# Four 16-bit score buffers instead of two for VectorE's exponentials, longer GpSimd products in the plan, and a new order

## The chip, the cores and the metric

The kernel runs on one core of a Trainium2 chip. A core has five engines that run side by side, each with its own instruction stream executed in order: TensorE (PE, matrix multiply), VectorE (DVE), ScalarE (ACT, activation functions), GpSimd (POOL) and SyncE (SP, here only a queue that starts DMA transfers). Engines wait for each other through semaphores. Matmul results land in PSUM, eight banks of 2 KB per partition; everything else lives in SBUF. The metric is the device time of one execution in microseconds (us), the median of several runs. A profile records every instruction of one execution.

## The reference

Two layers, each an attention block and an MLP block, on one sequence of 2048 rows of 448 values, 16 heads of 28:

```python
def _A_ref(x, wqkv, wo):            # attention
    q, k, v = split(x @ wqkv)       # 16 heads of 28
    scores = einsum("bhqd,bhkd->bhqk", q, k) * (28 ** -0.5)
    p = softmax(scores, axis=-1)
    return merge(einsum("bhqk,bhkd->bhqd", p, v)) @ wo

def _B_ref(x, w1, w2, w3, w4):      # shift mixer and MLP
    h = gelu(layernorm(x) @ w1)     # tanh form
    hs = shift_rows(h in four column groups, by -1, +1, -2, +2) @ w2
    x1 = x + hs
    return x1 + gelu(layernorm(x1) @ w3) @ w4

for _ in range(2):
    x = x + _A_ref(layernorm(x), wqkv, wo)
    x = x + _B_ref(layernorm(x), w1, w2, w3, w4)
```

In total 2 x 16 x 2048 x 2048 exponentials are needed, and they are the largest elementwise job of the program.

## The kernel before, in words

**Tiles.** The sequence is 16 row tiles of 128. Queries are cut into chunks of 4, 4, 4, 2 and 2 tiles (`CHUNKS`), heads into four groups `g` of four. A *segment* is one chunk, one head group and a range of key tiles; `ORDER` lists the ranges, for layer 0 `(0, 0, 4), (1, 0, 4), (0, 4, 8), (0, 8, 16), (1, 4, 16), (2, 0, 16), ...`, each for four head groups. There are 68 segments. A *block* is one 512-column score tile (128 keys by 512 query columns, of one head, or two key tiles by 256 columns in the short chunks); there are 2048 blocks.

**Exponentials on two engines.** `t_scores` groups blocks into units. TensorE writes the scores of a unit into banks 0 to 2 or 3 to 4 (5 at times), and one ScalarE instruction (line 1754, in `t_exp`) computes the exponential of two or three blocks at once into the ring `PT`. Some blocks go to VectorE instead. `ahead_of` chooses one from 5 to 9 steps further on, if the planner's rates (`R_RATE`, `D_RATE`, one entry for two segments) allow it and if a `y` buffer, a `pd` buffer and a bank are free at once (`"try"`). `d_first` (line 1584) reads the scores from PSUM into a 16-bit integer tile `y`; `d_chain` (lines 1611 to 1624) then computes the exponential from integer and bf16 operations, seven instructions on 512 columns, each dependent on one before it. Its scratch is an `f` buffer (2 KB, shared with other work: normalization and gelu) and, before the change, the second half of the 2 KB `y` buffer, which holds the tile `w`. While parts of the value store `vaug` are still unused, its slots serve as further buffers (`xtra`, `t_extra`).

**After the scores.** `t_pv` multiplies the exponentials with the values into one bank (line 831); at the end of each segment VectorE copies or adds the sum into `ub` (lines 1838 and 1840). `t_norm` brings the row sums by DMA to one tile, takes reciprocals, broadcasts them back by DMA into an `f` buffer (line 1861) and multiplies (`otn`, line 1865). `t_outproj`, `t_mixA`, `t_mixB` and `t_w4` do the output projection and the mixer and MLP of the finished rows beside the attention of the next chunks. What they still have to do for the last chunks runs after the last exponential; the second row group of the MLP there is tiles 11 and 12, the third 13 to 15.

**Products on GpSimd or VectorE.** `both(key, pool_dur, dve_dur, ...)` places a product of two SBUF tiles by `XPAR[key]`: 1 for VectorE, 0 for GpSimd, 2 for the one that would end it first by the plan. This holds for `otn` (key `eo`), the squares of queries and keys (`eq`, `ek`), the squares in gelu (`ez`, line 2034) and the addition `x_res + x1b` (`ex`, line 2120).

**The order.** No order is written by hand. Every piece of work is a Python generator, and `Sched.run` picks the next instruction of each engine at build time, with a planned duration for each, ranks (`RANK`, and `dp`, `rp` in `XPAR`), leads (`Q_LEAD`) and thresholds (`dt`, `wt`, `ft`). `after_lock` keeps a VectorE instruction marked `two` and a long GpSimd product from overlapping in the plan. Where the plan leaves TensorE a gap, `keep_pe_busy` puts in filler matmuls (line 2267) that no result depends on. `Plan.finalize` turns dependencies into semaphore waits. The engines then execute their lists in that order, whatever the real durations are.

## Time and profile before

| | before |
|---|---|
| median of 3 runs | 1025.69 us (1025.05 to 1025.9) |
| profiled execution | 1025.66 us |
| its span | 1023.9 us |
| instructions | 36349 |
| TensorE busy | 973.4 us, 95% |
| ScalarE busy | 973.6 us, 95% |
| VectorE busy | 843.5 us, 82% |
| GpSimd busy | 220.1 us, 21% |
| exponentials on ScalarE (line 1754) | 791 instructions, 877.8 us |
| score tiles read by VectorE (line 1584) | 94 into `yd`, 40 into `vaug` |
| filler matmuls | 2508 |

In a row of the groups stand: source line, engine, operation, what is written and read, count, then total busy time, mean duration of one in ns, and the idle time of the engine just before these instructions with what ended it. Durations of neighbours on one engine overlap a little, so a mean is longer than the step from one start to the next. In a row of the timeline stand start and length in us, and in brackets the idle time before it and its releaser. The granted TensorE clock is shown as a share of full speed.

### The profile page before, as it was taken

The numbers are of one execution on the slowest core, as the hardware profiler recorded it, in microseconds if no ns is written. First come the engines' busy times: TensorE is split into PE (matmuls) and PEld (weight loads), VectorE is DVE, ScalarE is ACT, GpSimd is POOL, SyncE is SP. The second block draws the span as 40 slices with busy tenths as digits, with TensorE's granted clock in tenths as the row PEclk, the third lists the DMA queues.
The fourth block names the chain that finished last, engine by engine and source line by source line (L and its number), as shares of the span: only waits on it lengthen the run. The fifth ranks groups of instructions, "written<-read, shape, count | busy, mean of one in ns | idle before, by whom it ended". The sixth has DMA issues, their size and how long they took to land.

```text
span 1023.9 us, 36349 instructions
## 1 busy us (share of the span) xinstructions
PE 973.4 (95%) x16102; PEld 404.7 (40%) x16102; DVE 843.5 (82%) x2134; ACT 973.6 (95%) x897; POOL 220.1 (21%) x350
## 2 busy tenths in 40 slices
PE   8999899999999999999999999999999999999998
PEld 4333344334343334344344333333333333444465
DVE  8879999988768778897788888997898888788752
ACT  6899999999999999999999999999999999999942
POOL 4003022143213013350212010112332200331220
PEclk9999999999999999999999999999999999999999
DMA  4534228121203113321133024324311110220000
GB/s 126 130 74 140 59 76 216 34 44 37 33 18 84 43 49 88 51 39 19 36 87 63 22 76 140 112 80 112 74 29 33 32 55 13 55 61 17 13 21 25
DMA packets 98829, 64.43 MB, mean 63 GB/s; under 512 B 70832, under 2 KB 87552, under 8 KB 98672
## 3 DMA queue, kind: packets, MB, share of 16 engines
q1 hardware_dynamic: 94176, 53.11, 21.1%
q0 software_dynamic: 3376, 8.09, 3.0%
q8 instruction: 126, 2.06, 0.9%
q10 hardware_dynamic: 1120, 0.92, 0.3%
q14 instruction: 31, 0.25, 0.1%
HBM read 28.16 MB, written 16.76 MB: 44 GB/s over the span
## 4 chain that ended last, share of the span: by engine, by line
ACT 62%; PE 23%; DVE 12%; DMA 1%; issue 1%; ACTq 0%; SPq 0%; DVEq 0%
ACT PT L1754 55%; PE ps L840 12%; PE ps L1487 5%; PE ps L831 4%; ACT h2T L2220 3%; PE ps L2267 1%; ACT fb L2036 1%; DVE yd L1584 1%; DMA xT<-xnd 1%; DVE fb L1619 1%; DVE fb L1615 1%; DVE PD L1624 1%; DVE ub L1840 1%; DVE vaug L1621 1%; ACT L1754 1%
## 5 line engine op out<-in xcount | busy, mean ns | idle before, releaser
L1754 ACT ACTIVATE PT<-ps 128x1024 bf16<-128x1024 f32 (+1 forms) x791 | 877.8, 1288 | 7.8 <-PE ps L1487 6.6
L1487 PE MATMUL ps<-qT,kT 32*128 32x512 bf16 (+1 forms) x2560 | 310.1, 340 | 23.5 <-ACT PT L1754 17.7
L831 PE MATMUL ps<-PT,vaug 128*32 128x512 bf16 (+1 forms) x2396 | 243.8, 341 | 0.5 <-ACT PT L1754 0.3
L1487 PEld LDWEIGHTS ps<-qT,kT 32*128 32x128 bf16 x2560 | 79.7, 91 | 292.0 <-ACT PT L1754 262.9
L840 PE MATMUL ps<-xT,w 128*32 128x512 bf16 (+3 forms) x2592 | 178.7, 343 | 1.7 <-issue 0.8
L2267 PE MATMUL ps<-ident 128*32 128x256 bf16 x2508 | 123.0, 280 | 2.2 <-POOL ident L930 1.5
L831 PEld LDWEIGHTS ps<-PT,vaug 128*32 128x32 bf16 x2396 | 71.8, 94 | 91.5 <-issue 78.2
L840 PE MATMUL ps<-w,h2T 128*32 128x448 bf16 x1288 | 89.5, 355 | 2.0 <-ACT h2T L2220 2.0
L840 PEld LDWEIGHTS ps<-xT,w 128*32 128x32 bf16 (+1 forms) x2592 | 68.9, 95 | 52.5 <-issue 25.1
L2267 PEld LDWEIGHTS ps<-ident 128*32 128x32 bf16 x2508 | 73.1, 98 | 25.3 <-issue 9.2
L1584 DVE TENSOR_SCALAR yd<-ps 128x512 int16<-128x512 f32 x94 | 64.5, 686 | 21.8 <-PE ps L1487 21.1
L1865 POOL TENSOR_TENSOR otn<-ub,fb 128x512 bf16<-128x512 f32 (+1 forms) x32 | 37.2, 1162 | 189.3 <-DMA fb<-rscr 178.7
L2196 DVE CAST h2T<-ps 128x384 bf16<-128x384 f32 (+1 forms) x84 | 52.0, 619 | 19.7 <-PE ps L840 17.9
L1615 DVE TENSOR_TENSOR fb<-fb 128x512 bf16<-128x512 int16 x112 | 49.0, 438 | 0.7
L840 PEld LDWEIGHTS ps<-w,h2T 128*32 128x32 bf16 x1288 | 34.6, 96 | 31.0 <-issue 12.0
L831 PE MATMUL ps<-PD,vaug 128*32 128x512 bf16 (+1 forms) x146 | 43.9, 342 | 1.2 <-DVE PD L1624 1.0
L840 PE MATMUL ps<-xT,wk_pad 128*32 128x512 bf16 (+1 forms) x512 | 41.2, 369 | 1.8 <-DVE kT L1226 1.2
L2267 PE MATMUL ps<-ident,xn 128*32 128x256 bf16 x896 | 40.8, 274 | 0.6 <-DVE ub L1840 0.6
L840 PE MATMUL ps<-wo_pad,otn 128*32 128x448 bf16 x512 | 36.9, 355 | 3.2 <-DVE x_res L1920 1.7
L1621 DVE TENSOR_TENSOR yd<-yd,fb 128x512 int16<-128x512 int16 x88 | 38.3, 436 | 1.2
L840 PE MATMUL ps<-wv,xT 128*32 128x448 bf16 x480 | 37.7, 356 | 0.6 <-ACT kT L1227 0.2
L840 PE MATMUL ps<-xT,wq_pad 128*32 128x512 bf16 x448 | 36.8, 382 | 1.4 <-DVE kT L1226 0.8
(238 smaller groups left out, 1318.0 us busy)
## 6 DMA issues: line engine op xcount, KB each, us to landing
uscr<-ub SPq DMA_DIRECT2D x28, 256.0 KB
ub<-uscr SPq DMA_DIRECT2D x28, 256.0 KB
fb<-rscr SPq DMA_DIRECT2D x96, 64.0 KB, 2.1
xnd<-xn SPq DMA_DIRECT2D x28, 128.0 KB, 3.1
x_res<-in_A_x_dram POOLq DMA_DIRECT2D x16, 224.0 KB, 3.3
xd<-x_res SPq DMA_DIRECT2D x16, 224.0 KB, 2.3
x_res<-xd SPq DMA_DIRECT2D x16, 224.0 KB, 4.1
out_dram<-obf SPq DMA_DIRECT2D x16, 112.0 KB, 1.8
```

Of the source, the lines that this page charges most:

```text
L831: return lambda e: e.matmul(out=out, lhsT=lhsT, rhs=rhs, start=start, stop=stop, **kw)
L840: r.append(e.matmul(out=out[c:c + w, :], lhsT=lhsT[:, c:c + w], rhs=rhs, start=start, stop=stop, tile_position=(0, c)))
L1487: yield op("pe", (0.005 + NW * 0.00042) / nc_, lambda e, i=i, kc=kc, j=j, g=g, a=a, NW=NW, bank=bank: e.matmul(out=ps[:, bank, i * NW:(i + ...
L1584: yield op("dve", c_ps(512), lambda e: e.tensor_scalar(out=y.bitcast(I16)[:, 0:512], in0=ps[:, bi(bank), :], scalar1=SCALE * L2E * FS, sca ...
L1615: yield op("dve", D_[2], lambda e: e.tensor_tensor(out=z, in0=qa, in1=qa, op=ALU.mult), reads=fk, writes=fk, urge=urge, two=True)
L1619: yield op("dve", D_[4], lambda e: e.tensor_tensor(out=z, in0=z, in1=w, op=ALU.mult), reads=yk + fk, writes=fk, urge=urge, two=True)
L1621: yield op("dve", D_[5], lambda e: e.tensor_tensor(out=ya, in0=ya, in1=z, op=ALU.add), reads=yk + fk, writes=yk, urge=urge, two=True)
L1754: yield op("act", 0.0635 + n * w * 0.000833, lambda e, bk=bk, s0=s0, n=n, w=w: e.activation(out=PT[:, s0:s0 + n, 0:w], in_=ps[:, bk[0]:bk[ ...
L1865: yield both(("eo", L, ch), 0.2 + NW * 0.0021, 0.07 + NW * 0.00104, lambda e: e.tensor_tensor(out=otn[:, g, 0:NW], in0=u, in1=rb[:, 0:NW], ...
L2196: ev = op("dve", c_ps(m * NW), lambda e, hr=hr, pv=pv: e.tensor_copy(out=hr, in_=pv), reads=[("ps", bi(b))], writes=hk, touch=[b])
L2220: yield op("act", c_act(len(fr_) * NW), lambda e, v=v: e.activation(out=v, in_=v, func=ACT.Gelu_apprx_tanh), reads=allk, writes=allk, tab= ...
L2267: return [e.matmul(out=ps[32 * c:32 * c + 32, bi(b), 0:256].rearrange("p (a n) -> p a n", n=128), lhsT=xn[:, 0, D:D + 32] if live else ide ...
```

## The change

The `y` buffer is now just the 16-bit score tile, 1 KB, and there are four of them in the memory of two. The tile `w` moves into the first half of the `f` buffer, over the integer tile `qa` it is made from; for that the square `z = qa * qa` is taken first. The unused `vaug` slots give two 1 KB `y` buffers and two `f` buffers, where they gave two 2 KB `y` and one `f`. Three planned GpSimd durations get longer. The planner's tables (rates, ranks, leads, placements, thresholds) are replaced, which gives a new order on every engine. The computation is the same.

```diff
-R_RATE = {(0,): 0, (1,): 0.006, (2,): 0.016, (3,): 0.04, ...
+R_RATE = {(0,): 0.22, (1,): 0.006, (2,): 0.028, (3,): 0.11, ...
-RANK = {..., ('b', 0, 0): 2.161, ..., ('a', 0, 0): 1.465, ..., ('v', 0, 1): 1, ...
+RANK = {..., ('b', 0, 0): 2.386, ..., ('a', 0, 0): 2.501, ..., ('v', 0, 1): 2.032, ...
-Q_LEAD = {(0, 1): 7, (0, 2): 102, (0, 3): 50, (1, 0): 86, (1, 1): 54, (1, 2): 9, (1, 3): 71}
+Q_LEAD = {(0, 1): 27, (0, 2): 89, (0, 3): 44, (1, 0): 93, (1, 1): 51, (1, 2): 6, (1, 3): 13}
-D_RATE = {(0,): 0, (1,): 0.177, (2,): 0, (3,): 0.517, (4,): 0.133, (5,): 0.289, ...
+D_RATE = {(0,): 0, (1,): 0, (2,): 0, (3,): 0.517, (4,): 0.133, (5,): 0.398, ...
-XPAR = {'l0': 10, 'l1': 13, 'l2': 16, ..., ('eo', 0, 0): 2, ('eo', 0, 1): 2, ('eo', 0, 2): 0, ..., ('eq', 0, 2): 0, ...
+XPAR = {'l0': 10, 'l1': 13, 'l2': 17, ..., ('eo', 0, 0): 1, ('eo', 0, 1): 1, ('eo', 0, 2): 1, ..., ('eq', 0, 2): 1, ...
...
-        yd = sb("yd", [128, 2, 512], I32)
+        yd = sb("yd", [128, 4, 512], I16)
...
-                    return {"y": ["yv%d" % base, "yv%d" % (base + 2)], "f": ["fv%d" % (base + 4)], "pd": ["pv%d" % (base + 6)]}[kind]
+                    return {"y": ["yv%d" % base, "yv%d" % (base + 1)], "f": ["fv%d" % (base + 2), "fv%d" % (base + 4)], "pd": ["pv%d" % (base + 6)]}[kind]
...
-        YS = ["y0", "y1"]
+        YS = ["y0", "y1", "y2", "y3"]
...
-            ya, yu, w = y.bitcast(I16)[:, 0:512], y.bitcast(U16)[:, 0:512], y.bitcast(BF16)[:, 512:1024]
+            ya, yu = y, y.bitcast(U16)
...
-            qu, qa, z = q.bitcast(U16)[:, 0:512], q.bitcast(I16)[:, 0:512], q.bitcast(BF16)[:, 512:1024]
+            qu, qa, w, z = q.bitcast(U16)[:, 0:512], q.bitcast(I16)[:, 0:512], q.bitcast(BF16)[:, 0:512], q.bitcast(BF16)[:, 512:1024]
...
+            yield op("dve", D_[2], lambda e: e.tensor_tensor(out=z, in0=qa, in1=qa, op=ALU.mult),
+                     reads=fk, writes=fk, urge=urge, two=True)
             yield op("dve", D_[1], lambda e: e.tensor_scalar(out=w, in0=qa, scalar1=EA / 65536.0, scalar2=EB, op0=ALU.mult, op1=ALU.add),
-                     reads=fk, writes=yk, urge=urge, two=True)
-            yield op("dve", D_[2], lambda e: e.tensor_tensor(out=z, in0=qa, in1=qa, op=ALU.mult),
                      reads=fk, writes=fk, urge=urge, two=True)
...
-                yield both(("eo", L, ch), 0.2 + NW * 0.0021, 0.07 + NW * 0.00104, ...
+                yield both(("eo", L, ch), 0.2 + NW * 0.00225, 0.07 + NW * 0.00104, ...
...
-            yield both(("ez", L, t0), 0.2 + NW * 0.00165, 0.07 + NW * 0.00104, ...
+            yield both(("ez", L, t0), 0.2 + NW * 0.00207, 0.07 + NW * 0.00104, ...
...
-            yield both(("ex", L, t), 1.2, 0.54, ...
+            yield both(("ex", L, t), 1.25, 0.54, ...
```

24 lines of the change are left out of this document (12 added, 12 removed).

## Prediction

> **What bounds the kernel now.** First the page: busy shares, then the chain that ended last, then the costliest group, then the filler group.
>
> ```profile
> PE 973.4 (95%) x16102; PEld 404.7 (40%) x16102; DVE 843.5 (82%) x2134; ACT 973.6 (95%) x897; POOL 220.1 (21%) x350
> ACT 62%; PE 23%; DVE 12%; DMA 1%; issue 1%; ACTq 0%; SPq 0%; DVEq 0%
> L1754 ACT ACTIVATE PT<-ps 128x1024 bf16<-128x1024 f32 (+1 forms) x791 | 877.8, 1288 | 7.8 <-PE ps L1487 6.6
> L2267 PE MATMUL ps<-ident 128*32 128x256 bf16 x2508 | 123.0, 280 | 2.2 <-POOL ident L930 1.5
> ```
>
> TensorE and ScalarE are both at 95%, but 2508 of TensorE's matmuls only fill its waits (L2267). The chain is ScalarE's for 62%, nearly all exponentials (L1754). So I cut the span where ScalarE's steady stream begins and where the last exponential ends.
>
> ```profile
> 0.00:33.07 33.07, 28.03 (x461) 13.62 (x461) 28.41 (x94) 20.99 (x30) 10.70 (x24) 1.00 0.40 121
> 33.07:970.47 937.40, 895.71 (x14472) 359.25 (x14472) 795.39 (x2000) 932.56 (x840) 202.58 (x311) 1.00 0.26 63
> 970.47:1023.90 53.43, 49.68 (x1169) 31.81 (x1169) 19.73 (x42) 20.07 (x29) 6.79 (x15) 1.00 0.09 25
> ```
>
> Columns: stretch, its length, then busy time of PE, PEld, DVE, ACT, POOL, then PE's clock. In the middle ScalarE works 932.56 of 937.40 us: 4.84 us idle in all. The last 53.43 us are TensorE's (49.68 busy). So the time is a head, ScalarE's work plus its few waits, and TensorE's tail. The profiled execution took 1025.66 us, 1.76 around its span of 1023.9; the median of the three runs is 1025.69, so the sum against 1025.66 needs no correction. A measurement of this kernel tells about 0.2%, 2.05 us, from no change.
>
> **The change, part by part.** It is mostly a new plan, so I counted instructions in both built programs.
>
> *Exponentials.* Despite four buffers, VectorE takes fewer score tiles: 130 instead of 134. ScalarE has 474 two-tile exponentials for 459, 323 three-tile for 332, and one single. All its other instructions, 16 table loads too, keep their number. The head's order on ScalarE is unchanged.
>
> ```profile
> L1754 ACT ACTIVATE PT<-ps 128x1536 bf16<-128x1536 f32 x332 | 503.2, 1540 | 5.9 <-PE ps L1487 5.3
> L1754 ACT ACTIVATE PT<-ps 128x1024 bf16<-128x1024 f32 x459 | 482.3, 1106 | 1.8 <-PE ps L1487 1.3
> 522.16 1.34 ACT PT L1754
> 526.37 0.91 ACT PT L1754
> ```
>
> The means, 1540 and 1106 ns, overlap their neighbours; on the chain of waits one costs 1.34 and 0.91. A tile is 0.43, so a single is about 0.48. Sum: 15 x 0.91 - 9 x 1.34 + 0.48 = 13.65 - 12.06 + 0.48 = +2.1; with 1.35 for a three-tile one, +2.0. I take +2.0, all on the path.
>
> *Tail.* Before:
>
> ```profile
> 970.64 0.49 PE L2267 MATMUL ps<-ident 128*32 128x256 bf16 x8
> 972.54 0.62 PE L2267 MATMUL ps<-ident 128*32 128x256 bf16 x13
> 975.27 1.05 PE L840 MATMUL ps<-xT,w 128*32 128x256 bf16 x32
> 978.15 1.51 PE L840 MATMUL ps<-w,kT 128*32 128x448 bf16 x28 [0.50 <-ACT kT L2220]
> 992.11 5.42 PE L840 MATMUL ps<-xT,w 128*32 128x256 bf16 x192
> 997.35 0.93 PE L840 MATMUL ps<-w,h2T 128*32 128x448 bf16 x16
> ```
>
> After the last exponential TensorE fills (36 matmuls between 970.64 and 973) until the last output projection can start; at 978.15 ScalarE's wide gelu ends, and from there TensorE runs to the end almost without a gap. Among that work are the 192 first-layer MLP matmuls (L840, 256 wide) of tiles 11 and 12, 5.24 us from start to start, 27.3 ns each. In the changed order 28 of the group's 224 stand ahead of the last scores, 84 take the fillers' place, 12 stand beside the gelu, and 76 + 20 + 4 = 100 are left behind it: 92 fewer, 92 x 0.0273 = -2.5. The gelu chain in front keeps its instructions. Bounds: 0 if a new dependency stalls the tail as long; -3.1 if everything taken from behind the output projection counts, 192 + 32 - 112 = 112 matmuls. I take -2.5, since the one gap the rows show there is 0.50.
>
> *GpSimd products.* They cost the plan more (0.00225 for 0.0021 us a column for `otn`, 0.00207 for 0.00165 for the squares in gelu, 1.25 for 1.2), and 27 move to VectorE: 8 + 4 + 8 + 5 + 2. In layer 0 no 512-wide `otn` and no `sq<-qT` square stays on GpSimd. GpSimd's own time is off the path. What matters is this:
>
> ```profile
> 140.10 1.05 DVE yd L1613
> 141.17 1.40 DVE fb L1615
> 153.49 0.81 DVE vaug L1621
> 172.16 1.36 DVE L1624 TENSOR_SCALAR PD<-yd 128x512 uint16<-128x512 uint16 x1
> 175.16 0.29 DVE L1624 TENSOR_SCALAR PD<-yd 128x512 uint16<-128x512 uint16 x1
> 190.91 1.33 DVE L1212 TENSOR_TENSOR sq<-qT 128x512 bf16<-128x512 bf16 x1
> 171.94 1.43 POOL L1865 TENSOR_TENSOR otn<-ub,fb 128x512 bf16<-128x512 f32 x1 [2.37 <-DMA fb<-rscr]
> 190.66 1.30 POOL L1865 TENSOR_TENSOR otn<-ub,fb 128x512 bf16<-128x512 f32 x1
> 174.44 1.02 ACT L1754 ACTIVATE PT<-ps 128x1024 bf16<-128x1024 f32 x1 [0.55 <-PE ps L1487]
> 175.76 16.78 ACT L1754 ACTIVATE PT<-ps 128x1536 bf16<-128x1536 f32 x14 [0.29 <-PE ps L1487]
> 193.06 15.56 ACT L1754 ACTIVATE PT<-ps 128x1024 bf16<-128x1024 f32 x14 [0.53 <-PE ps L1487]
> ```
>
> The first three rows are from the chain of waits, the others from the timelines. The same VectorE instruction takes 0.29 us alone and 1.36 while a GpSimd product runs; both VectorE rows with a product beside them end when it ends, and within two to three microseconds ScalarE waits for scores. [...]
>
> ```profile
> 112.82:163.47 50.65, 46.45 (x779) 19.84 (x776) 48.53 (x129) 50.62 (x45) 13.22 (x16) 1.00 0.38 111
> 163.47:246.98 83.51, 77.52 (x1248) 32.41 (x1248) 75.41 (x188) 81.67 (x75) 22.57 (x32) 1.00 0.30 67
> ```
>
> (Stretches between the attention sums' copies that end a chunk's part, `(0, 8, 16)` and `(1, 4, 16)` of layer 0.) ScalarE idles 1.84 us in the second and 0.03 in the first. If the holds go, the second comes near the first: I take -1.7. Bounds: 0 if something else is late next, -4.84 if all of the middle's idle time goes.
>
> *VectorE's price for it.* Here the orders differ most.
>
> ```profile
> L1584 DVE TENSOR_SCALAR yd<-ps 128x512 int16<-128x512 f32 x94 | 64.5, 686 | 21.8 <-PE ps L1487 21.1
> L1615 DVE TENSOR_TENSOR fb<-fb 128x512 bf16<-128x512 int16 x112 | 49.0, 438 | 0.7
> L1617 DVE TENSOR_SCALAR fb<-fb 128x512 bf16<-128x512 bf16 x112 | 34.4, 308 | 0.8
> L1212 DVE TENSOR_TENSOR sq<-qT 128x512 bf16<-128x512 bf16 x14 | 7.0, 501 | 0.3
> L1865 DVE TENSOR_TENSOR otn<-ub,fb 128x512 bf16<-128x512 f32 x4 | 2.7, 684 | 0.0
> L2034 DVE TENSOR_TENSOR fb<-hT 112x512 f32<-112x512 bf16 x2 | 1.4, 692 | 0.1
> ```
>
> A chain instruction is 0.36 (four of the 308 kind, three of the 438 kind, over seven). Between the same copies the changed order has, in the first stretch, 12 chain instructions, one score read (0.69), three squares (1.50) and two `otn` (1.37) more, one bias addition (0.68) and two memsets (1.2) fewer: 4.3 + 0.7 + 1.5 + 1.4 - 1.9 = +6.0, so 54.5 us of work in 50.65. In the second: 7 chain instructions fewer (-2.5), five `otn` (3.4), four gelu squares (2.8) and three others (1.7) more: +5.4, 80.8 in 83.5. But the 48.53 and 75.41 contain the holds. The three shown for the first stretch lasted 1.05, 1.40 and 0.81 where their kinds take 0.31, 0.44 and 0.44: 2.1 us; the two in the second cost 1.07 and 0.83. Without them 52.4 is wanted in 50.65 and 78.9 in 83.5: over by 1.8 in the first, under by 4.6 in the second. I put it at 0, since score tiles are taken ahead of their use and the second stretch can take what runs over; the other end, no relief at all, is 54.5 - 50.65 = +3.9.
>
> *Moved or added waits.*
>
> ```profile
> POOL otn L1865 <- DMA fb<-rscr: 178.7, 19, 36.2
> DVE xn L1065 <- POOL rstd L1058: 2.8, 4, 1.1
> 153.95 0.81 POOL L880 DMA_DIRECT2D w<-in_B_w_dram  x1
> 257.70 0.56 DVE L2196 CAST h2T<-ps 128x384 bf16<-128x384 f32 x1 [0.26 <-PE ps L840]
> ```
>
> An `otn` product waits for a broadcast by DMA, on GpSimd for 178.7 us at no cost. On VectorE the same wait would hold the chains, evacuations and score reads queued behind it, and TensorE with them. The four that stood there before waited 0.0, so I take 0; the upper bound is VectorE's largest sum of waits for an engine other than TensorE, +2.8. The MLP weights' load (L880) moves one segment later, some 21 us (83.51 / 4), and past other GpSimd loads; its first reader comes at 257.70, 104 us after its issue, which leaves some 80; without that cover it would cost up to 21. The 435 SyncE transfers stay in number; their readers have the same kind of slack: 0. The chain's `w` in the other buffer, the swapped second and third step and the smaller tile cost 0: seven instructions on the same 512 columns, each still behind the last. The 31 groups of fillers that go (2508 to 2380, and one more of the other kind) cost 0, since they stand in waits.
>
> Sum: 1025.66 + 2.0 - 2.5 - 1.7 = 1023.46, forecast 1023.5.
>
> **Rivals.**
> *No change, 1025.2.* The holds go, but VectorE's extra work makes as much delay, or they only move to layer 1, where GpSimd keeps its products. For it: 2.0 and 2.5 nearly cancel, and 52.4 us in 50.65 leaves VectorE no rest. Against it: ScalarE lost 0.03 us beside VectorE at 48.53 of 50.65. Then 1025.66 + 2.0 - 2.5 = 1025.2. That the buffers don't do what they say belongs here: twice as many, and fewer tiles.
>
> *Slower, 1029.0.* VectorE becomes the bound between 112 and 163 us. It decides from the point where its work exceeds the stretch, that is if less than 3.9 us of holds go. Every copy of an attention sum then comes late, TensorE's next products wait for it, and scores queue behind them: 1025.66 + 2.0 - 2.5 + 3.9 = 1029.0. For it: +6.0 us in a stretch already 96% full (48.53 of 50.65), where the chain runs through VectorE's rows. Against it: the 2.1 us of holds shown, whose products leave.
>
> *Faster still, 1020.3.* Every wait of ScalarE in the middle comes from a hold, and all 4.84 us go: 1025.66 + 2.0 - 2.5 - 4.84 = 1020.3. For it: the three waits shown. Against it: GpSimd keeps 12 of the 512-wide `otn` products in layer 1.
>
> **How the numbers follow.** Forecast 0.35; faster still 0.05; no change 0.34; VectorE bound 0.26. So faster 0.40, same 0.34, slower 0.26. The range runs from 1019.7 (the last case with -3.1 for the tail) to the slow case with a third of the broadcasts' 2.8 us on top, 1030.0; the likeliest case alone has 1021.5 to 1024.5, the cases faster and no change together most of the chance.
>
> **What would show it.** Right: L1754 474 and 323 times; under 0.5 us of ScalarE idle around the second chunk's attention; no chain instruction on VectorE over 1 us in layer 0; some 51 us behind the last exponential. Wrong: VectorE above 98% with ScalarE idle beside it there, `otn` on VectorE waiting for its DMA, a tail of 53 us or more with a gap ahead of its hT matmuls, or a TensorE clock below the 1.00 of every row above.

## The result and the profile after

The changed kernel takes 1030.1 us (median of 4 runs, 1029.24 to 1031.24); the kernel before takes 1025.78 beside it. The ratio is 1.0043, 95% interval 1.0029 to 1.0056: slower by 4.3 us, where 1023.5 was forecast. The profiled execution is the slowest of the four, 1031.24 us with a span of 1029.0, against 1025.66 and 1023.9 before.

The page of the changed kernel, the same four lines as before:

```profile
PE 978.8 (95%) x15975; PEld 405.8 (39%) x15978; DVE 843.2 (82%) x2129; ACT 976.2 (95%) x904; POOL 185.3 (18%) x323
ACT 63%; PE 32%; DVE 4%; DMA 1%; issue 0%; SPq 0%; DVEq 0%
L1754 ACT ACTIVATE PT<-ps 128x1024 bf16<-128x1024 f32 (+1 forms) x798 | 881.7, 1286 | 10.6 <-PE ps L1487 9.3
L2267 PE MATMUL ps<-ident 128*32 128x256 bf16 x2380 | 115.2, 281 | 1.6 <-POOL ident L930 1.5
```

GpSimd has lost 34.8 us of work, VectorE is as busy as before, and ScalarE's wait ahead of the exponentials has grown from 7.8 to 10.6 us. The chain that ended last runs through TensorE for 32% of the span where it was 23%, and through VectorE for 4% instead of 12%. The cuts of the prediction, put where the same instructions stand (ScalarE's steady stream begins 2.24 us later here, the last exponential ends at 978.12):

```profile
0.00:35.31 35.31, 28.61 (x458) 14.18 (x461) 28.51 (x94) 20.98 (x30) 10.78 (x24) 0.95 0.38 114
35.31:978.12 942.81, 902.69 (x14423) 361.53 (x14426) 795.82 (x1996) 935.09 (x848) 167.57 (x284) 0.99 0.25 63
978.12:1029.00 50.88, 47.49 (x1102) 30.10 (x1093) 18.91 (x40) 20.08 (x29) 6.95 (x15) 1.00 0.07 23
```

Against 33.07, 937.40 and 53.43 the head is 2.24 longer, the middle 5.41, the tail 2.55 shorter; 0.48 comes from outside the span (2.24 instead of 1.76). Together 5.58, which is 1031.24 - 1025.66. In the middle ScalarE is busy 2.53 us more (935.09 for 932.56) and idle 2.88 us more (7.72 for 4.84).

The new thing in these rows is the clock: 0.95 and 0.99, where each row of before has 1.00. Cut finer, the loss lies in three places. First a stretch with little TensorE work, then the stretch behind it (for the head only the latter):

```profile
9.90:13.30 3.40, 3.18 (x46) 1.80 (x49) 2.97 (x17) 0.85 (x2) 1.57 (x3) 0.50 0.53 166
186.80:190.20 3.40, 1.44 (x12) 0.41 (x15) 3.39 (x12) 3.36 (x4) 0.00 (x0) 1.00 0.00 0
190.80:194.20 3.40, 3.40 (x29) 0.80 (x29) 2.38 (x6) 3.06 (x3) 1.88 (x4) 0.50 0.02 5
687.00:690.40 3.40, 1.72 (x15) 0.37 (x15) 3.40 (x8) 2.67 (x3) 1.11 (x2) 0.82 0.27 77
690.40:695.40 5.00, 4.86 (x36) 1.08 (x36) 2.99 (x9) 2.73 (x3) 0.00 (x0) 0.50 0.23 68
```

From 186.8 us TensorE works 1.44 of 3.4 us, and from 190.8 on its clock is 0.50; ScalarE beside it works 3.06 of 3.40. From 687 it is 1.72; the clock falls at 689.14 and stays at half for 6.8 us, and in 5.00 of these ScalarE works 2.73. The timeline of the changed kernel shows how each place comes about (TensorE at 188 to 194 us, then VectorE, GpSimd, TensorE and ScalarE at 684 to 696 us):

```profile
188.46 0.39 PE L1487 MATMUL ps<-qT,kT 32*128 32x512 bf16 x3 [1.10 <-ACT PT L1754]
189.37 0.39 PE L1487 MATMUL ps<-qT,kT 32*128 32x512 bf16 x2 [0.52 <-ACT PT L1754]
...
192.73 1.65 PE L840 MATMUL ps<-wo_pad,otn 128*32 128x448 bf16 x16
...
684.69 1.26 DVE L1613 TENSOR_TENSOR fb<-fb 128x512 bf16<-128x512 int16 x1
685.87 1.48 DVE L1621 TENSOR_TENSOR yd<-yd,vaug 128x512 int16<-128x512 int16 x1
...
684.52 1.15 POOL L1212 TENSOR_TENSOR sq<-qT 128x512 bf16<-128x512 bf16 x1 [47.35 <-DVE qT L1288]
685.63 1.44 POOL L1865 TENSOR_TENSOR otn<-ub,fb 128x512 bf16<-128x512 f32 x1
...
688.36 0.40 PE L840 MATMUL ps<-sq,astatq 128*32 128x512 bf16 x4 [1.54 <-DVE qT L1288]
...
689.37 1.45 ACT L1754 ACTIVATE PT<-ps 128x1536 bf16<-128x1536 f32 x1 [0.73 <-PE ps L1487]
691.74 1.02 ACT L1754 ACTIVATE PT<-ps 128x1024 bf16<-128x1024 f32 x1 [0.92 <-PE ps L1487]
694.11 1.45 ACT L1754 ACTIVATE PT<-ps 128x1536 bf16<-128x1536 f32 x1 [1.34 <-PE ps L1487]
696.04 4.62 ACT L1754 ACTIVATE PT<-ps 128x1024 bf16<-128x1024 f32 x4 [0.48 <-PE ps L1487]
```

At 187 us TensorE waits for ScalarE, twice, and no filler stands in the wait; behind it 16 output-projection matmuls take 1.65 us (0.93 for 16 of them at 185.45, at full clock). At 684 us two GpSimd products hold two VectorE steps to 1.26 and 1.48 us, the copy of `qT` behind them comes late, TensorE waits 1.54 us for it, and 0.8 us after it goes on its clock falls to half: ScalarE waits four times, 3.47 us in all. In the kernel before, TensorE lacks work near both places as well, but there fillers stand in the waits: 0.73 of the 2.23 us that it works from 189.0 on, and 2.10 of 3.14 from 683.9 on. The filler line alone (L2267), before and then after:

```profile
189.00:192.40 3.40, 0.73 (x20) 0.44 (x20) 1.00 0.04 7
683.90:687.30 3.40, 2.10 (x36) 0.77 (x33) 1.00 0.18 64
```

```profile
186.80:190.20 3.40, 0.00 (x0) 0.00 (x0) 1.00 0.00 0
```

In the changed kernel no filler stands between 684 and 688.4 us either.

In the changed kernel's trace the clock has two values, 1.00 and 0.50 (0.82, 0.95 and 0.99 above are means of stretches that hold both). At 0.50 it stays for 3.41 us from 9.89 and from 190.80 us, and for 6.83 us from 689.14. TensorE was not idle ahead of the falls: it was at work for 1.44 and 1.72 of 3.4 us. When the falls come is taken up below (products put back).

### The profile page after: what moved, and what is told of

It is laid out like the page before. It is cut to its first block, busy times and chain, and to the rows that moved or that the text cites. A ratio compares the mean times of both kernels' runs of the same rounds, so it can differ in the third digit from the quotient of the medians.

```text
span 1029.0 us, 36049 instructions
## 1 busy us (share of the span) xinstructions
PE 978.8 (95%) x15975; PEld 405.8 (39%) x15978; DVE 843.2 (82%) x2129; ACT 976.2 (95%) x904; POOL 185.3 (18%) x323
## 4 chain that ended last, share of the span: by engine, by line
ACT 63%; PE 32%; DVE 4%; DMA 1%; issue 0%; SPq 0%; DVEq 0%
ACT PT L1754 56%; PE ps L840 17%; PE ps L1487 8%; PE ps L831 6%; ACT h2T L2220 3%; PE ps L2267 1%; ACT L1754 1%; ACT fb L2036 1%; ACT hT L2018 1%; DMA h2T<-in_A_x_dram 1%; ACT L2018 0%; DVE h2T L2196 0%; ACT L2220 0%; DVE xn L1065 0%; ACT vaug L2220 0%
## 5 line engine op out<-in xcount | busy, mean ns | idle before, releaser
L1754 ACT ACTIVATE PT<-ps 128x1024 bf16<-128x1024 f32 (+1 forms) x798 | 881.7, 1286 | 10.6 <-PE ps L1487 9.3
L1487 PE MATMUL ps<-qT,kT 32*128 32x512 bf16 (+1 forms) x2560 | 313.9, 341 | 23.4 <-ACT PT L1754 17.8
L840 PE MATMUL ps<-xT,w 128*32 128x512 bf16 (+4 forms) x2592 | 181.0, 344 | 1.3 <-DVE h2T L2196 1.1
L2267 PE MATMUL ps<-ident 128*32 128x256 bf16 x2380 | 115.2, 281 | 1.6 <-POOL ident L930 1.5
L1584 DVE TENSOR_SCALAR yd<-ps 128x512 int16<-128x512 f32 x105 | 72.2, 688 | 23.1 <-PE ps L1487 21.6
L2267 PEld LDWEIGHTS ps<-ident 128*32 128x32 bf16 x2380 | 69.7, 99 | 23.4 <-issue 8.5
L1865 POOL TENSOR_TENSOR otn<-ub,fb 128x256 bf16<-128x256 f32 (+1 forms) x24 | 25.3, 1054 | 158.2 <-DMA fb<-rscr 140.5
L1613 DVE TENSOR_TENSOR fb<-fb 128x512 bf16<-128x512 int16 x97 | 44.1, 461 | 0.7
L2267 PE MATMUL ps<-ident,xn 128*32 128x256 bf16 x900 | 44.0, 274 | 0.3 <-DVE ub L1840 0.2
L1619 DVE TENSOR_TENSOR fb<-fb 128x512 bf16<-128x512 bf16 x97 | 40.3, 419 | 1.0
```

The costliest lines, as they stand in the source:

```text
L840: r.append(e.matmul(out=out[c:c + w, :], lhsT=lhsT[:, c:c + w], rhs=rhs, start=start, stop=stop, tile_position=(0, c)))
L1487: yield op("pe", (0.005 + NW * 0.00042) / nc_, lambda e, i=i, kc=kc, j=j, g=g, a=a, NW=NW, bank=bank: e.matmul(out=ps[:, bank, i * NW:(i + ...
L1584: yield op("dve", c_ps(512), lambda e: e.tensor_scalar(out=y, in0=ps[:, bi(bank), :], scalar1=SCALE * L2E * FS, scalar2=-126.0 * FS, op0=A ...
L1613: yield op("dve", D_[2], lambda e: e.tensor_tensor(out=z, in0=qa, in1=qa, op=ALU.mult), reads=fk, writes=fk, urge=urge, two=True)
L1619: yield op("dve", D_[4], lambda e: e.tensor_tensor(out=z, in0=z, in1=w, op=ALU.mult), reads=fk, writes=fk, urge=urge, two=True)
L1754: yield op("act", 0.0635 + n * w * 0.000833, lambda e, bk=bk, s0=s0, n=n, w=w: e.activation(out=PT[:, s0:s0 + n, 0:w], in_=ps[:, bk[0]:bk[ ...
```

## The experiments

Theory: the half clock makes the difference, it follows stretches in which TensorE has little to do, and those come from VectorE held by GpSimd (684 us) and from a wait in which no filler stands (187 us). Rivals: VectorE's lateness itself costs the time and the clock only goes with it; VectorE's added products are what is late; the buffers or the order cost by themselves.

Except for the two halves of the change, each kernel is the planned list played once more with a small edit, so that nothing else moves. `("pe", 28)` is entry 28 of TensorE's list; an entry is up to four matmuls. `blank(i)` is four filler matmuls into bank i, `zeros(i)` four matmuls that add zero to bank i while it holds results. `move` gives an entry to another engine at its place in the plan, `insert` puts entries behind one, `sooner` puts an entry further ahead, `drop` leaves it out. The kernel before ran beside each group, and a ratio is to its median there: 1025.17 us beside the first four kernels below, 1025.89 beside the next four (up to the first half of the change), 1025.79 beside the second half and the three kernels after it, 1025.59 beside the last three. Times of different groups are best compared by their ratios.

### Fillers in the head

```diff
+    insert["pe", 28] = [blank(0)] * 8
+    insert["pe", 41] = [blank(0)] * 3
+    insert["pe", 45] = [blank(0)] * 3
```

> The changed kernel with 14 groups of four filler matmuls more before 10.2 us (8 ahead of the first transposes, 3 ahead of the second, 3 ahead of the row-sum matmul); everything else stands as it was. Clock theory: in the changed kernel TensorE was busy for only 1.89 of the 3.4 us from 6.8 us on, and the clock then stood at 0.50 from 9.9 to 13.2 us; filled, the clock stays at 1.00 there, ScalarE's exponentials start 2.2 us earlier (29.7 instead of 31.97 us for the instruction at that place), and the time falls by about 2.2 us, 1030.1 to 1027.9. Rival, late data: the fourth tile of x came 1.15 us later by DMA and TensorE would have waited all the same; then the fillers change nothing, 1030.1. Rival, chance: the fall at the head is that one execution's; then this run's time is about that of the changed kernel and its profile differs by itself.

Measured: 1029.14 us, ratio 1.0034 (1.0022 to 1.0047). The clock is 1.00 throughout the first 33 us, but the instruction in question starts at 30.64, not 29.7. ScalarE's row here, in the changed kernel, and in a kernel whose head is unedited and whose clock did not fall there (the one with products put back, below):

```profile
30.64 2.37 ACT L1754 ACTIVATE PT<-ps 128x1536 bf16<-128x1536 f32 x2 [2.75 <-PE ps L1487]
```

```profile
31.97 2.37 ACT L1754 ACTIVATE PT<-ps 128x1536 bf16<-128x1536 f32 x2 [2.75 <-PE ps L1487]
```

```profile
29.55 2.36 ACT L1754 ACTIVATE PT<-ps 128x1536 bf16<-128x1536 f32 x2 [2.75 <-PE ps L1487]
```

So in the profile of the changed kernel the head lost 2.4 us (31.97 - 29.55), half of which came back: the added fillers cost 1.1 themselves. The fall there does not come from the new order: of the eight profiles below whose head is that of the changed kernel, two have it, and up to there TensorE, ScalarE, VectorE and GpSimd have the same order in the kernel before. How often each kernel has it is not shown, since a run without a profile gives only its mean clock.

### Matmuls that add zero at 187 us

```diff
+    insert["pe", 1263] = [zeros(4)] * 6
+    insert["pe", 1266] = [zeros(2)] * 2
+    insert["pe", 1268] = [zeros(4)] * 3
```

> The changed kernel with 11 groups of four matmuls that add zero to score banks, put into TensorE's waits between 187.3 and 190 us; everything else stands as it was. Clock theory: TensorE was busy 1.43 of the 3.4 us from 186.8 us on and the clock then stood at 0.50 from 191 to 194.3 us; with 1.2 us of matmuls more in that stretch the clock stays at 1.00, the 16 output-projection matmuls at 192.7 us take 0.93 instead of 1.65 us, the 0.89 us of ScalarE's wait at 194.75 us goes, and the time falls by 0.9 to 1.7 us, to about 1029. Rival, VectorE: the stretch is late because VectorE's copy of the attention sum is late (189.25 us); then ScalarE's wait and the time stay, 1030.1.

Measured: 1027.24 us, ratio 1.0016 (1.0007 to 1.0025). The windows of this kernel at the same place:

```profile
184.50:187.90 3.40, 2.88 (x59) 1.24 (x59) 3.37 (x12) 3.40 (x3) 0.00 (x0) 1.00 0.00 0
188.50:191.90 3.40, 3.40 (x48) 1.14 (x49) 3.33 (x9) 3.40 (x4) 1.68 (x4) 1.00 0.04 10
```

2.88 us instead of 1.44, the clock stays, and ScalarE works through. VectorE is as busy (3.37). Between 183.5 and 197.5 us ScalarE now idles 0.04 us; in the changed kernel, between 186 and 200, it was 0.93. That the whole gain is larger than this isn't this place's doing: the head kept its clock in this profile too.

### Matmuls that add zero at 687 us

```diff
+    insert["pe", 5159] = [zeros(7)] * 13
```

> The changed kernel with 13 groups of four matmuls that add zero to the attention-sum bank, put into the one wait of TensorE at 686.8 to 688.36 us; everything else stands as it was, GpSimd's products and VectorE's held instructions too. Clock theory: the clock stays at 1.00 from 690 to 695.5 us; ScalarE's waits of 0.92, 1.34 and 0.48 us after 691 go and only the 0.73 at 689.4 us, which VectorE's late copy of q makes, stays; the time falls by about 2.7 us, to 1027.4. Rival, the holds: VectorE's two instructions of 1.26 and 1.48 us beside GpSimd's products make all four waits; then nothing changes, 1030.1.

Measured: 1027.07 us, ratio 1.0017 (1.0008 to 1.0026). ScalarE's rows of this kernel:

```profile
689.18 1.45 ACT L1754 ACTIVATE PT<-ps 128x1536 bf16<-128x1536 f32 x1 [0.71 <-PE ps L1487]
691.14 1.02 ACT L1754 ACTIVATE PT<-ps 128x1024 bf16<-128x1024 f32 x1 [0.51 <-PE ps L1487]
692.44 13.66 ACT L1754 ACTIVATE PT<-ps 128x1536 bf16<-128x1536 f32 x12 [0.28 <-PE ps L1487]
```

VectorE's steps are held as before and the 0.71 stays; of 3.47 us of waits 1.50 are left. The other 2.0 were the clock's. The rival (all of it the holds') falls, but 0.8 us more than I expected belong to the hold. (This profile is the slowest of the eleven runs, 1029.04 us; its clock fell in the head and at 187 us.)

### The three products at 684 us on VectorE

```diff
+    move.update({("pool", n): "dve" for n in (205, 206, 207)})
```

> The changed kernel with the three GpSimd products at 684.5, 685.6 and 688.3 us done by VectorE at the same place of the plan; no filler is added and nothing else moves. Both theories expect TensorE's wait of 1.54 us to shrink, since VectorE gives up 1.9 us of holds for 1.7 us of products and gets its 128x512 steps of the exponentials back to 0.42 us. If the wait falls below about 1 us the clock theory expects 1.00 through 695 us and 3.5 us less, 1026.6; the hold theory expects 0.7 to 1 us less, 1029.2. If VectorE's own load is what is late, nothing changes or it gets slower, 1030 to 1031.

Measured: 1025.14 us, ratio 1.0002 (0.9993 to 1.0011), 1.5 us better than expected. VectorE's steps that were held, and then all that ScalarE still waits there:

```profile
683.12 0.42 DVE L1613 TENSOR_TENSOR fb<-fb 128x512 bf16<-128x512 int16 x1
683.45 0.42 DVE L1621 TENSOR_TENSOR yd<-yd,vaug 128x512 int16<-128x512 int16 x1
...
687.68 1.02 ACT L1754 ACTIVATE PT<-ps 128x1024 bf16<-128x1024 f32 x1 [0.20 <-PE ps L1487]
688.98 16.41 ACT L1754 ACTIVATE PT<-ps 128x1536 bf16<-128x1536 f32 x15 [0.28 <-PE ps L1487]
```

1.26 and 1.48 us have become 0.42 each; 0.48 us of waits are left. Moving three products, with no other change, takes back 3.0 us of ScalarE's waits there (3.47 to 0.48): the hold, and the fall behind it. The rest of the difference between the two profiles is not this edit's: the head kept its clock in this one, and at 187 us it fell as before. VectorE can carry the three products.

### All three edits

```diff
+    insert["pe", 28] = [blank(0)] * 8
+    insert["pe", 41] = [blank(0)] * 3
+    insert["pe", 45] = [blank(0)] * 3
+    insert["pe", 1263] = [zeros(4)] * 6
+    insert["pe", 1266] = [zeros(2)] * 2
+    insert["pe", 1268] = [zeros(4)] * 3
+    move.update({("pool", n): "dve" for n in (205, 206, 207)})
```

> The changed kernel with three edits together: the fillers in the head, the matmuls that add zero in the waits at 187 to 190 us, and the three GpSimd products at 684 to 688 us done by VectorE. Clock theory: no stretch of 3.4 us is left in which TensorE is busy for less than 2 us, the clock is 1.00 in every row as in the kernel before, and the time is what the prediction's sum gave, 1023.5 us (1023 to 1024), 1.5 us below the kernel before on this chip (1025.2). Rival: each fall of the clock hides behind a lateness of VectorE that stays, so that the gains don't add up; then about the 1025.1 of the run with the products moved alone.

Measured: 1025.33 us, ratio 0.9999 (0.9990 to 1.0007). The clock is 1.00, but the fillers in the head cost their 1.1 us here as well (the instruction that starts at 29.55 without them starts at 30.69), so this is no better than the three products alone. The number is the rival's, but not for the rival's reason: the gains do add up in ScalarE's idle time (0.04 us at 187 us, 0.49 at 684).

### Products put back to GpSimd at 171 to 181 us

```diff
+    move.update({("dve", n): "pool" for n in (427, 433, 446)})
```

> The changed kernel with three products (the otn at 171.4 and 181.3 us and the square of q at 174.1 us) put back from VectorE to GpSimd at the same place of the plan; nothing else moves. VectorE theory (its extra products make the attention sum's copy at 189.25 us late): VectorE has 1.8 us less to do before that copy; if the products are not held against it, the copy comes up to 1.8 us earlier, TensorE's waits of 1.10, 0.52 and 0.29 us go, the clock stays at 1.00 from 191 us on and the time falls by 0.9 to 1.7 us, to 1028.4 to 1029.2. Hold theory (a GpSimd product costs VectorE more than doing it): three VectorE steps of 0.28 to 0.42 us become 1.1 to 1.4 us, the copy is as late or up to 1.2 us later, and the time stays at 1030 to 1031.

Measured: 1029.27 us, ratio 1.0030 (1.0021 to 1.0040). VectorE's copy of the sum is as late as it was (186.93 us in this execution, whose head is 2.4 us shorter), so the products that the change moved to VectorE are not what is late at 187 us, and neither theory's numbers came. Nor did these products hold VectorE much: one stretched a step of 0.42 us to 0.84, one ran while VectorE waited for TensorE, and beside the one at 176.31 us two score reads took 1.28 us together, as they did without it. The surprise is the profiled execution itself:

```profile
184.40:187.80 3.40, 1.43 (x12) 0.36 (x15) 3.40 (x13) 3.36 (x4) 0.00 (x0) 1.00 0.99 306
189.81 0.94 PE L840 MATMUL ps<-wo_pad,otn 128*32 128x448 bf16 x16
...
683.80:687.20 3.40, 1.36 (x15) 0.35 (x15) 3.40 (x8) 2.69 (x3) 1.20 (x2) 1.00 0.23 77
687.20:692.20 5.00, 4.74 (x64) 1.59 (x64) 4.85 (x11) 4.22 (x5) 1.04 (x1) 1.00 0.19 59
...
32.90:972.55 939.65, 899.35 (x14423) 360.90 (x14426) 794.27 (x1993) 935.02 (x846) 172.72 (x287) 1.00 0.25 63
```

The same thin stretches, 1.43 and 1.36 of 3.4 us, and this time the clock did not fall. The trace of this execution has no clock rows at all, so the 1.00 in it is no measurement; the matmuls show the full clock, for 16 of the output projection take 0.94 us behind the first stretch, where they took 1.65 at half clock. That execution took 1025.47 us. The other nine runs of the same program, by their mean clock: 0.995 in six, 1028.47 to 1029.52 us; 0.993 in three, 1029.64 to 1030.67. One program, one order, and the time goes with the clock, though with one run at the full clock: the clearest reading of the study, and it came unplanned.

The traces also suggest what the chance is. In all five executions with several falls they lie on a grid: in the changed kernel they begin at 9.89, 190.80 and 689.14 us, which is 53 and then 146 steps of 3.413 us, and each lasts one or two steps. Where the grid lies differs from execution to execution: in the profile of the changed kernel run once more (below) a fall begins at 689.93 us, where this grid has one point at 689.14 and the next at 692.55. So I take it that what counts is how much work lies between two grid points, and not in the thinnest 3.4 us; the steps of the profiles, in the last section, agree with that in part. In the changed kernel the two steps ahead of the falls are thin:

```profile
187.38:190.79 3.41, 1.47 (x16) 0.39 (x16) 3.34 (x12) 3.41 (x4) 0.07 (x1) 1.00 0.00 0
685.73:689.14 3.41, 1.87 (x20) 0.53 (x18) 3.41 (x6) 2.91 (x3) 2.19 (x2) 1.00 0.26 75
```

In the execution that kept its clock a grid point would cut the first thin stretch in two. (Its grid is an estimate: its first 100 fillers take 4.78 us, against 4.68 and 4.88 in two executions whose clock first rises at 5.18 and 5.59 us, so it rises at about 5.4.)

```profile
182.88:186.30 3.42, 2.27 (x30) 0.74 (x28) 3.42 (x15) 3.38 (x4) 0.00 (x0) 1.00 1.02 304
186.30:189.71 3.41, 2.55 (x26) 0.61 (x23) 3.31 (x10) 3.41 (x4) 1.20 (x2) 1.00 0.89 293
```

By the same estimate its step at 684 us holds 2.00 us.

### The kernel before with 19 groups of fillers left out

```diff
+    drop.update(("pe", n) for n in (3911, 3912, 3917, 3918, 3919, 3920, 3925, 6474, 6476, 6477, 6478, 6479, 6484, 6485, 6490, 6491, 6492, 6493, 6498))
```

> The kernel before, with the 19 groups of filler matmuls between 500.4 and 504.5 us and between 865.1 and 870.1 us left out; everything else in its old order. In these two stretches TensorE was busy for 2.17 and 2.19 of 3.4 us, about 1.0 us of it fillers. Clock theory: with some 1.2 of 3.4 us left the clock falls to 0.50 for 3.4 us behind each, ScalarE waits for scores, and the time rises by 1 to 3.5 us, from 1025.2 to 1026.2 to 1028.7. The prediction's step (fillers cost nothing, since they stand in waits, and leaving them out costs nothing either): 1025.2, clock 1.00.

Measured: 1025.82 us, ratio 1.0003 (0.9994 to 1.0012).

```profile
500.20:503.60 3.40, 1.33 (x28) 0.45 (x24) 3.09 (x8) 3.40 (x1) 1.56 (x4) 1.00 0.00 0
865.60:869.00 3.40, 1.44 (x24) 0.43 (x20) 3.39 (x10) 3.39 (x2) 0.00 (x0) 1.00 0.01 1
```

TensorE's work fell to 1.33 and 1.44 us as meant. In this execution the clock stayed; in 5 of the 11 runs it was 0.998, which is what one fall of 3.4 us makes of the mean (half of 3.4 in 1024 us is 0.0017), against 1 of 26 of the kernel before beside them. Four of the five are no slower than the six at 1.00 (1025.28, 1025.51, 1025.82 and 1026.66, among 1024.62 to 1027.03), one is (1029.13). ScalarE is in a gelu of 6.2 us at both places and needs nothing from TensorE, which would explain why a fall costs nothing there; but the profile is of a run without one, so where the clock fell in the five is not shown. Here the prediction's step holds: fillers left out cost nothing.

### The two halves of the change alone

The buffers, the chain and the `vaug` slots with the old tables:

```diff
-        yd = sb("yd", [128, 2, 512], I32)
+        yd = sb("yd", [128, 4, 512], I16)
...
-        YS = ["y0", "y1"]
+        YS = ["y0", "y1", "y2", "y3"]
```

> The kernel before with the buffer part of the change alone: four 1 KB score buffers, the tile w in the f buffer, and the vaug slots as two y and two f buffers; the planner's tables and durations are the old ones, so the order is planned anew from tables that were not made for it. If the buffers were what the change gains by, this is at or below the kernel before, 1025 us or less. If the order is what counts, it is slower by some microseconds, 1028 to 1040, with the clock falling in places.

Measured: 1040.58 us, ratio 1.0143 (1.0124 to 1.0161), at a clock of 1.00. The new tables and durations with the old buffers:

```diff
-XPAR = {'l0': 10, 'l1': 13, 'l2': 16, ...
+XPAR = {'l0': 10, 'l1': 13, 'l2': 17, ...
...
-                yield both(("eo", L, ch), 0.2 + NW * 0.0021, 0.07 + NW * 0.00104, ...
+                yield both(("eo", L, ch), 0.2 + NW * 0.00225, 0.07 + NW * 0.00104, ...
```

> The kernel before with the planner's tables and the three longer GpSimd durations of the change, and with the two old 2 KB score buffers: the other half of the change alone, planned anew. If the new order is good by itself, this is 1026 to 1031 like the changed kernel. If tables and buffers only fit together, it is slower by 5 to 20 us, as the buffers alone were (1040.6).

Measured: 1039.90 us, ratio 1.0138 (1.0119 to 1.0156). Neither half is any good alone: a set of tables fits one set of buffers. What the buffers are worth can't be told from this.

### The changed kernel once more

```diff
+# the changed kernel once more
```

> The changed kernel once more, unedited. Clock theory: the falls of the clock behind 187 and 687 us come in most executions and the one in the head in some, so that the median is 4 to 4.5 us above the kernel before, with granted clocks of 0.993 to 0.995; an execution with a clock of 1.00, if there is one, takes 1025 to 1026 us. Rival, the slowness is not the clock's: the times do not follow the clock.

Measured: 1030.04 us, ratio 1.0040 (1.0026 to 1.0054), clocks of 0.993 and 0.995 in five runs. In its profile the clock fell behind 187 and 687 us and not in the head, as the theory has it.

### Zeros at 187 us and four products on VectorE

```diff
+    insert["pe", 1263] = [zeros(4)] * 6
+    insert["pe", 1266] = [zeros(2)] * 2
+    insert["pe", 1268] = [zeros(4)] * 3
+    move.update({("pool", n): "dve" for n in (205, 206, 207, 249)})
```

> The changed kernel with the matmuls that add zero in the waits at 187 to 190 us and with four GpSimd products done by VectorE at the same place of the plan: the three at 684 to 688 us and the otn at 805.4 us, beside which a VectorE step of the exponentials took 0.96 instead of 0.42 us and behind which ScalarE waited 0.51 us; no filler is added in the head. Clock and hold theory: ScalarE's idle time in the middle falls from 7.7 us to about 3.4, the clock is 1.00, and without the 1.1 us that the added fillers of the head cost, the time is 1.5 us below the kernel before: 1024. Rival: ScalarE's own longer list (busy 2.3 us more than before in the middle) eats what the tail brings; then 1025, no difference from the kernel before.

Measured: 1024.42 us, ratio 0.9991 (0.9982 to 1.0000), with the prediction's three stretches:

```profile
0.00:32.91 32.91, 27.34 (x461) 13.35 (x461) 28.24 (x94) 20.95 (x30) 10.73 (x24) 1.00 0.39 122
32.91:971.13 938.22, 899.95 (x14467) 361.78 (x14470) 793.95 (x2000) 934.85 (x847) 163.01 (x280) 1.00 0.25 63
971.13:1022.10 50.97, 47.49 (x1102) 30.14 (x1091) 18.91 (x40) 20.10 (x29) 6.96 (x15) 1.00 0.07 23
```

With the falls and the holds at 684 and 805 us gone it is 1.4 us below the kernel before beside it, where the sum had 2.2. That is an edited kernel, with four products on VectorE that the changed one leaves on GpSimd. Six of its runs have a clock of 1.00 and take 1024.06 to 1024.42; five have 0.998 and take 1025.63 to 1026.18.

### Two products of the kernel before on VectorE

```diff
+    move.update({("pool", n): "dve" for n in (52, 55)})
```

> The kernel before with the two otn products at 171.9 and 190.7 us moved from GpSimd to VectorE at the same place of the plan; nothing else moves. This is the prediction's step for the products alone: the held VectorE steps of 1.36 and 1.33 us go, ScalarE's waits of 0.55, 0.29 and 0.53 us behind them go, and the time falls by 1 to 1.4 us. Rival, VectorE's own load: the two products take VectorE 0.68 us each, as long as the holds cost it on balance (1.07 and 0.83 us), its copies are as late, and nothing changes (within 0.3 us).

Measured: 1023.43 us, ratio 0.9978 (0.9969 to 0.9987), all eleven runs at a clock of 1.00 and within 1023.01 to 1023.83. By its median it is the fastest kernel of the study, ahead of both.

```profile
33.05:968.44 935.39, 895.80 (x14472) 359.45 (x14472) 794.97 (x2002) 932.17 (x841) 199.58 (x309) 1.00 0.26 63
...
159.79 47.07 ACT L1754 ACTIVATE PT<-ps 128x1024 bf16<-128x1024 f32 x41
```

ScalarE now runs from 159.79 to 206.86 us without a wait, where it had waited 0.55, 0.29 and 0.53 us; its idle time in the middle is 3.22 us instead of 4.84. The two products take VectorE 0.69 us each, less than the 1.07 and 0.83 us that their holds cost it.

### The late copy put ahead

```diff
+    sooner["dve", 473] = ("dve", 461)
+    sooner.update({("pe", n): ("pe", 1263) for n in (1269, 1270, 1271, 1272, 1273, 1274)})
+    sooner.update({("pe", n): ("pe", 1266) for n in (1275, 1276, 1280, 1281, 1282, 1283)})
```

> The changed kernel with VectorE's copy of the attention sum, which stood at 189.25 us behind twelve more steps of the exponentials, put ahead of those twelve, and with twelve of the next segment's attention products on TensorE put ahead of the scores that wait for ScalarE (six behind the scores at 187 us, six behind those at 188.5 us). No filler is added and no work is moved to another engine. Order theory (the copy is late because the score tiles that VectorE took ahead stand in front of it): TensorE's busy time in the 3.4 us from 186.8 us on rises from 1.43 to about 2.1 us, the clock stays at 1.00 there, ScalarE's waits between 190 and 197 us (0.7 to 1.3 us) go, and the time falls by 0.7 to 1.5 us, to about 1029. Rival, ScalarE's slowness there is the clock's phase alone: nothing changes, 1030.

In this kernel and the next, up to four of the attention products put ahead no longer wait for VectorE's last step on their tile, so both times are those of kernels that wait for less than they must. Measured: 1028.58 us, ratio 1.0028 (1.0016 to 1.0039).

```profile
186.60:190.00 3.40, 1.88 (x20) 0.40 (x14) 3.33 (x12) 3.40 (x4) 0.96 (x2) 1.00 0.02 5
190.00:194.00 4.00, 3.92 (x32) 0.97 (x32) 2.87 (x8) 3.08 (x3) 0.98 (x3) 0.57 0.00 0
```

1.88 instead of the 2.1 us expected, and the clock fell behind it. The edit did not do what the order theory needs: what is put ahead is missing later, and TensorE then waits for ScalarE all the same. There is too little TensorE work at this place, and nothing fills it.

### The late copy put ahead, and four products on VectorE

```diff
+    sooner["dve", 473] = ("dve", 461)
+    sooner.update({("pe", n): ("pe", 1263) for n in (1269, 1270, 1271, 1272, 1273, 1274)})
+    sooner.update({("pe", n): ("pe", 1266) for n in (1275, 1276, 1280, 1281, 1282, 1283)})
+    move.update({("pool", n): "dve" for n in (205, 206, 207, 249)})
```

> The changed kernel with the edit of the copy and the attention products at 187 us, and with four GpSimd products (684.5, 685.6, 688.3 and 805.4 us) done by VectorE; no filler is added. Both causes taken away at their origin and not covered up: clock 1.00, time as with the added zeros and the same four products, 1024.4 (1024 to 1024.8), 1 to 1.5 us below the kernel before. Rival, the order edit costs VectorE's chains what it gains TensorE: 1025 or more.

Measured: 1026.18 us, ratio 1.0004 (0.9993 to 1.0015), with clocks from 0.995 to 1.000. Its clock fell at 187 us in the profile, for 6.8 us. Taking away the origin as I saw it does not give what the added zeros gave (1024.42).

### Three products of the kernel before on VectorE

```diff
+    move.update({("pool", n): "dve" for n in (52, 55, 56)})
```

> The kernel before with three otn products moved from GpSimd to VectorE at the same place of the plan: the two at 171.9 and 190.7 us as before, and the next one, beside which a VectorE step took 1.38 us at 198.8 us. Hold theory: the third hold goes too, ScalarE's wait of 0.28 us at 207.1 us with it, and the time is 0.3 us below that with two products (1023.4), 2.4 us below the kernel before. Rival: VectorE has other work behind which that wait comes anyway; then as with two.

Measured: 1024.09 us, ratio 0.9982 (0.9974 to 0.9991). Not better than two; with these intervals it cannot be told from it. ScalarE's wait of 0.28 us at 207 us went, and one of 0.37 us at 214 us came in its place. So the gain does not go on with each hold that is moved.

## Why the prediction was wrong

**Exponentials, +2.0: right.** The counts came as said:

```profile
L1754 ACT ACTIVATE PT<-ps 128x1024 bf16<-128x1024 f32 x474 | 502.5, 1111 | 3.4 <-PE ps L1487 2.9
L1754 ACT ACTIVATE PT<-ps 128x1536 bf16<-128x1536 f32 x323 | 497.6, 1543 | 7.2 <-PE ps L1487 6.4
```

In the middle ScalarE is busy 2.5 us more (2.3 with zeros and four products).

**Tail, -2.5: right.** 53.43 became 50.88, and 50.97 with zeros and four products.

**GpSimd products, -1.7: the mechanism right, the term about -0.2.** Moving two of them in the old order took ScalarE's idle time from 4.84 to 3.22 us, 1.6 us, and the time by 2.4. In the changed order the holds of layer 0 are gone as well. But the rival "they only move to layer 1" was right at the same time: in the kernel before 11 chain steps of VectorE last over 1 us, 5 of them in layer 0; in the changed kernel it is 12, none before 580 us. In the execution that kept its clock ScalarE idles 4.63 us in the middle (939.65 - 935.02), 0.2 less than before, and its 1025.47 us are that rival's 1025.2. Two of the products, at 684 us, hold VectorE just where TensorE waits for it, 1.0 us by themselves (1.50 us of waits with the gap filled, 0.48 with the products moved). I had looked only at the holds that go and not for those that come: which GpSimd products stand ahead of a copy that TensorE needs.

**VectorE's extra work, 0: right.** In the first stretch of the prediction, between the same copies, VectorE is busy 48.98 us in the changed kernel, hardly more than the 48.53 before and far from the 52.4 that the sum had wanted, and ScalarE does not wait at all:

```profile
115.90:166.74 50.84, 47.98 (x799) 21.30 (x799) 48.98 (x144) 50.84 (x47) 0.00 (x0) 1.00 0.20 55
```

Part of the 52.4 was counted too high, for mean durations overlap their neighbours; the rest is not explained. Three of the products put back changed nothing at 187 us, and three more taken over at 684 us cost nothing. At 187 us VectorE is at work for 3.39 of 3.40 us, with ScalarE short of scores a little later: what I had named as the sign of a VectorE bound. It was not the cause: with zeros put in, and in the execution that kept its clock, VectorE is as busy there and ScalarE idles 0.04 us.

**The fillers, 0: the step that failed.** I wrote that the fillers that go "cost 0, since they stand in waits". That is what they are for. A wait of TensorE without a filler isn't empty time only: where 1.4 to 2.0 of 3.4 us were work, the clock mostly fell to half behind it, and where ScalarE lives on TensorE's scores that cost 2.0 us at 687 us (a fall of 6.8 us) and 0.9 at 187 (one of 3.4 us: 0.93 us of idle time, 0.04 with the zeros). In the second profile of the changed kernel the long fall was the one at 187, and the costs were 1.5 and 1.5. With the hold's 1.0 these are 3.9 to 4.0, and 6.3 in an execution that has the head's 2.4 too; 5.7 lie between 1024.4 and 1030.1. So the order that was forecast at 1023.5 stands at 1025.47 in the one execution that kept its clock (with three products put back), 0.2 below the kernel before, and the falls put it 4.3 above. I had counted the fillers over the whole span and not looked where the new order leaves a thin place. The prediction names "a TensorE clock below the 1.00" among the things that would make it wrong, but gave it no chance and no price.

As a sum, for the kernel with zeros and four products: -0.16 for the head, +2.29 for ScalarE's work, -1.47 for its idle time, -2.46 for the tail and +0.37 outside the span make -1.43, that is 1024.23 in that profiled execution; the forecast was 1023.46. The slower rival gave 1029.0 by another road, VectorE as the bound between 112 and 163 us, and that did not happen; that it lies near the measured time is luck.

**What stays open.** Why the planner leaves TensorE without work or fillers at 187 us is not shown: three products put back left the copy as late, and the copy put ahead brought TensorE only 0.4 us more work in the stretch. And 0.3 to 0.5 us more lie outside the span in each newly planned program (2.24 and 2.04 in two executions of the changed kernel, 2.14 and 2.19 for the two halves, against 1.76 before and 1.79 with two products moved); no run here explains it.

## What to carry to other kernels

Before calling a filler or a gap free, slide a window of 3.4 us (the shortest falls here last 3.41) over TensorE's busy time and look for the thinnest stretches of the new order, and for what hangs on TensorE right behind them; in these kernels a gap cost something where ScalarE waited for scores and nothing was seen where it had a gelu of 6.2 us of its own. When products move between GpSimd and VectorE, follow the holds that arise as well as those that go: the two that counted here, at 684 us, stood just ahead of a copy for which TensorE waited 1.54 us. If runs of one program spread, sort them by the granted clock before looking for a cause in the order.

## What the runs showed of the hardware

The clock fell though TensorE was never idle for long (in the changed kernel its longest waits ahead of the three falls were 0.78, 1.10 and 1.54 us): behind 1.44 and 1.72 of 3.4 us of work in the changed kernel and behind 1.88 with the copy put ahead, and not behind 1.43 and 1.36 with products put back or 1.33 and 1.44 with fillers left out. The grid of 3.413 us agrees with much of this. In the 15 profiles with clock rows, counted from grid point to grid point, all six steps with 1.36 to 1.59 us of work were followed by a fall, of nine with 1.83 to 1.99 five were, and of the many with 2.0 to 2.5 four (in the kernel with fillers left out the grid cut the two stretches into steps of 2.13 and 2.20, and of 1.83 and 2.23, and nothing fell). So the boundary is not sharp by this measure. A fall lasted 3.4 us, or twice that. Matmuls that only add zero to a bank that holds results kept the clock up in the two places tried (2.88 of 3.4 us from 184.5 us on and 3.15 from 686.4, clock 1.00), which helps where no bank is free for a filler.

A GpSimd product of 1.1 to 1.4 us stretched VectorE's 0.42 us steps to 1.26 and 1.48, and the same product on VectorE took 0.42 to 0.69. What makes the hold is not shown here. Not every product holds: beside the one put back at 176.31 us, VectorE took 1.28 us for two reads of scores from PSUM, as without it. Where a product did hold VectorE, VectorE was quicker with it as its own work than beside it (in the kernel before 0.69 us each for two products, against holds of 1.07 and 0.83). The kernel's gain did not grow with each product moved: it took 1023.43 us with those two and 1024.09 with a third.
